# A linear recurrence with hash-routed experts on one core: the lower bound's load on ScalarE's queue, and a new order of emission

## The chip, the core and the metric

The kernel runs on one core of a Trainium2 chip. Five engines work from queues of their own: TensorE (PE in the profile, its weight loads PEld), VectorE (DVE), ScalarE (ACT), GpSimd (POOL) and SyncE (SP, which here only issues transfers). Each engine takes its instructions strictly in the order in which the program emitted them, and waits at one until what it needs is there. The metric is the device time of one execution in microseconds, taken as the median over several runs.

## What is computed

A gated recurrence runs over 4 batches of 5056 steps with 256 channels, and its output, 20224 rows of 256, goes through a mixture of 8 experts. The expert of a row is a hash of its token id, which comes down to the id modulo 8. Each expert is 256 to 1024, relu, 1024 to 256.

```python
sig = 1.0 / (1.0 + np.exp(-f_logit))
f = lower_bound[None, None, :] + (1.0 - lower_bound[None, None, :]) * sig
i = 1.0 - f
for t in range(S):
    h = f[:, t] * h + i[:, t] * x[:, t]
    y[:, t] = h
...
expert_idx = token_ids * np.int64(2654435761) % np.int64(E)
for e in range(E):
    mask = expert_idx == e
    xe = x[mask]
    h = np.maximum(xe @ w1[e], 0.0)
    out[mask] = h @ w2[e]
```

## The kernel before

**Blocks.** Time is cut into 24 blocks: 64, 128, five of 256, two of 128, twelve of 256, one of 128 and two of 64 steps, each for all four batches. For a block, f and x are loaded (`ldf`, `ldx`, lines 831 and 836 early, 1012 later, on SP), turned so that channels lie on partitions, gated (`sig`, `fg`), combined (`st`), scanned on VectorE (`sc`, line 902 early and 1105 later), turned back and copied into `yT`. Blocks 0 to 6 are turned on TensorE (`trf` and `trx`, line 872, `yt`, line 941, and the copies `ye`, lines 955 and 957); later blocks by VectorE's stream transposes. The gate of the early blocks needs `lb_col`, which `load_lb` (line 367) loads.

**Ranks.** A row goes to place expert × capacity + rank in a buffer `srt` in DRAM. Ranks are made in four ranges of columns of 128 tokens: 0 to 6 (blocks 0 and 1), 6 to 46 (blocks 2 to 6), 46 to 78 and 78 to 158. The token ids come by `ids0` to `ids6` (lines 346 and 351) for the first two ranges. `ra0` and `ra6` (lines 438 to 454) make one-hot columns and running sums on VectorE; `rpe` (lines 469 to 475) adds over partitions on TensorE; `rb` and `rc` (lines 480 to 490) give `pos_i`, the places.

**Scatter.** GpSimd writes the rows of a block into `srt` by `si`, one indirect DMA (line 709) for every 128 rows, 114 in all; for some of the later blocks half the rows are sorted on TensorE (line 733) and moved by SP instead. `fill` (line 390, SP) writes zeros into the tiles in the middle of `srt`, reads them from a tile that VectorE writes again in `zfd` (line 402) once the fill has landed, and waits for every scatter emitted ahead of it, since both write `srt`.

**Experts.** `srt` is read in 21 tiles of 128 rows per expert. A read (`rd`, line 1193, SP) needs the fill and the scatters of every block that can reach the tile; tile 0 needs blocks 0 to 2, tiles 2 and 3 need blocks up to 5 and 6, tile 20 block 23. A unit is two tiles (of one expert, or one tile of two experts): `up` (line 1203, TensorE), relu `re` (1212 on ScalarE or 1214 on VectorE), `dn` (1220, TensorE), a copy `oc` into one of four output buffers `ob` (1228 or 1230), and two stores `ro` (line 1234, GpSimd, indirect DMA to the output, 168 in all). The weights come by 16 loads of 0.5 MB from GpSimd's queue (lines 647 and 649; `lw3.1` is the first matrix of expert 3).

**Order.** Every step is a task with an engine and dependencies. The order in which the tasks are emitted, and with it the order in each engine's queue, is a string `ORDER` of 2159 task numbers with one bit that says, for relus, copies and gates that may run on either, whether VectorE takes it. `Plan.order` decodes it; priorities and durations in the tasks play no part then, and dependencies are enforced by semaphores as the instructions need them:

```python
for v in array("H", zlib.decompress(base64.b85decode(ORDER))):
    t = self.tasks[v & 0x7FFF]
    t.on = ("DVE" if v >> 15 else "ACT") if t.alt else next(iter(t.eng))
    out.append(t)
```

Of the kernel before, what the change touches and what calls it, by code (L numbers as in the profile page):

```python
# [55 lines left out]

ORDER = (
    "c-"
    "jTQ1Atvg5CFhYcTa5Fwr$(CZ6}vE*!>&Zwr$(CZQHsk8E}?}#bUKtTgF&B7KznmF<FeDJxj{!vs6Jx){u2zby#Osj~UjOMG3kDiCI_HfW>Emsh}T"
    "A$U3pqK_k{Ah{p!7xGV!p!kPw_bqo5lX2HOqdC-Ej3<j~-EDj4}6Iq&Ia1hQytb5>Ck05O@B=Br2Tgf7VOsprH%!URD*i<%xO<^O0xvUo(6-"  # L60
    ";8QS#mZySjC31`D_83793;KgBih^U@c3=Ua{BgKQ@nTW9x!e!A`b5*v>WtV_12%n=NEx*&eni$QbkvPO!|uE|w+O%Vx5B>?AwR76;kcl3*4~8JuG"
    "Kf(L8|Tgpna{lR?}upB{hzKop?va-HxBiqEX1rOPo;8Adiy<rD}$HCd)97`WuVL5|7Y#e*XuCmxXU2vIIU{8W;tTlTY#N{dYLDq&HV#8TMRwy_eT"
    "o2B(_iQ=)5WHnSSsb39-3V?5AA{fQFDu8MvG`^Mi)TIs$p5g<K`pNN7B-tbXTMkiGoH<1w-_<v|AN~rp-IV8@kAyvXC@La#0v!6Y-"
    "V{_6qA~#F=@>NR)l|HxmZ+_&U|G>c{W~{C+4|>Xh!fHJc$YC(Rnc*gGXk?O^Da#FIjdzf`4Nv0?F^P^kyV4Val=$rf_h9mE#q7)SwQ}$uF{4yrjv"
    "+%k$hOBX7y`25}%?5Wy?*q&$xq&Fk?>JQJ_Pj<URFH6P21u*#+`FB-"
    "g1aiNN7z+3ZVysD|s+nRwq9t`3QO(Ro`C5LEi6mP}H@c7Wi9ASg`MxKx7=b8CSUp!EJC<i{oykPCjCY}J=n>Box>0r9@|4cQ$mapfH%^g;eRc2Xu"
    "^kBG20qb~o-"
    "osQk385SB$eZw<{30*Fo0?L*6CY=KnUpYzPv*VNcvG5}2nzC4P=;lKKISUF#J@Ao6TxPl8cMRue72cr5`$*1RG6v3v%myihW}u*%oRSx#N<;=8b|"
    "^GpKmtsv{063<=1#kKEqt+H+eeXc8f_5QN?sK$L!#9c~!REY&G-"
    "vG_%0m;xWWRlNp+sjIhXT<2U#Lvy;D3yG&oc+blLSO+TIu3}0dnn%gETEH!!IkjV~vO+F|9#i0tz4|_}rNCtOJsh}WafI^T1DnenX#%jYI(}E|3!"  # L70
    "~CAvXZmx?kMNT4*c>&_cqu3X$4pKrFP53o5KUBq<K~TtEl!!I{G{p3%fJcq+T1q}%m7{%-to#1T`cEMOjCGns=!0@*1R`e_-FITy!MV)g>SqLd@="
    "Rlt*-_ZL`4xteC6fBR`HjnJ;W2S#7h3%d^B~T88qkB;ist&aYan=!Ze3mP)+<WJt4kr0F}gGC<-m00_-"
    ";*Om>^V{xTillSyuCz$<gc{N@dzC3J*V&<PTXM4~(tgGP`_C{dlY1|fRE3f>tK+mtq^$R$$PA&|tP$Y86BDxwdxftoA~qy<4DwXMOD+TM`E))2WN"
    "x9tn*Z8F;hx<VS82ZlmMQ45AaWid$P7u_I_&1?HXK06NngPPDE(%MX-rmZUe@LH^))#9`XAhS(p>)0V8tDOPEp)rI*2nLHLkj1uzY&HVM!#_R(ir"
    "ArI5fl{@pdA?KXorb4&;x3V0l-8p+gNn5BcYL<2*pGbF$wD0nJ@~5i+Z-"
    "H?PUM**{}_Y3k%I`ecRdoCrSzkB8foEg66iXwPG@~wB2keI|nw2?sha7u^38-C?c|$0!yKdZ7r6-T-"
    "Yw&sRPg*KB!jK+0x=19|+6f0v`n7Vw9Z+YvDX^YsW&E^>#U|gRx>gY=Cz56pRrKY{>Ss+o8Rk3T4D3y8^a~vwW%;0}ecNuv<g{v02QvJK(*aY?s@"
    "O5Mc|8f?_9Zf?aS0rig>^(XWIN_7Lob!*B#z*jaWn6cTU5G&{$RwsUPc(ZiM%dtjuUXXnFdI0Mt+EX=Uu>`|Bot6{p`B_`M%Vw*SzJH;`$3JdIby"
    "GU$>-QpUYhne;|%(pk-9&CX<b`>muh4zX)W7muQcCVdiFThQ>2rpo7*gkPi+=8oiA)FTn?0q<B--(CNUtG5<!~-~M--<)_B^-"
    "xO@Ceq3+pto+7X!sAam_x4Ug8z>5jX5-@m0KrBlecPV2|1-@CQDLoA$UEAl|@b$RIDlM{&u12EyLri}(s(;Gz9y`--*pqCIRsh-"  # L80
    "2b}eGC0WCixBi*}w4Jt`?uv5AhC8*`MO1jfG#-KiCH+;5(dzbz(o9w%KG7{AC&bws+wNaOCn1XuKmLVPw2*1-"
    "6ozWo!8qqF`+N>SMTc_}NRmZ2#Ej5EmbbpJ7?0aPJ{b_%nDW9@~vV;d7e<3t<_2BA(iea)Zb&Uy5q@0pf*gw?uq|7a}P#7Zqc<UqCJz{)YIN91~z"
    "NOo6dobWG~fV+>4*F<l&&5hKei@~@RH10u$AnQ*blDI>X<m_sU;3ZuB3*hXeXz_zlZ%#Cr~eG%2=!Yo)A^I$XwE@60knaeE`KU4x&1f#p6h%PVYa"
    "b+>SE97#!yfPoA#&)t8=5wiJ*6;?H9}{DFOePcIQc>8=l9gN$ncsa=<*+(dzyhw5OfE~i%B~frkf~)#xlqoL#c{4I<*Le`z9N>uF8ErMab;a+`AQ"
    "UZ9b^rx;%Z`AOe<?)IadiwVnNpszx#fe9n)YMIa@Zu#@Ga_xqG5Ew#GVmMK;A^E*qA{;aJ_3aK&8>SKhV3A+7)x#0su0{wIgYcG$&rb<PcS-"
    "DNZEitVv3cEggczFQ!>$p@koc1Q1exSp;DcEI7TGS+lqF2Ir4AFs-RI9~=XTpBk3dtyDTkBj6WG&oQ8!X(mSbL@zNG2|*bhokVWsDeYVmh0oL%XD"
    "%IPQ|J?8hg10a<LrYT3}zd#D$^9ezKt)6TVDFxZZe8j>T|nB$v9qZW^YS%jGXMAN$L3*b*1uD(vls;s7_ub;j{H0|&YlZjWmsJK+RuE)&Ye?v|X6"
    "`&|sR(yhk-a3O|pCT>OR63KnC5B9}vcvl{9iRBu1Th7A8xCocxAGHQYx!UrkT;-"
    "NvQ@6!U#C7ffuEW`QM;>y`<Zr(gZ^&VI(5=U17*mbFgSgcVcH3P9ZpZcVG|s^txYkX=ZElCFC&#;;xB++LNOuM+sg3y8PmsIt5XMvYTuV6_H@LZY"
    "7$3M@ZlZkX_TWx;1g~LTc@~$4-"  # L90
    "*=nB|EYPn(H+I>xZ3RvUx}OCL;UW};Wzi*RZ(^1Bb*|SVJx*DAGyOWwrU~I;~Sjnj^kT=<}TtS`PglCPh5Pp8CT#1yn#RDb2r(&b06I;{NOI(2|V"
    "d;;$wX3Udr3J4|ltt?uEO9-|-"
    "1nR!_02dWKstp?Z#Yak`u)kI2j6qvbpNf$#B^dx0!0f%@cLyL<S?jg=oTj{4$WVl5>pu8Kwp=#>2DPT^1d<xV>eC-IN_h*$8p`-"
    "NxZIXOnYbq_F+Pvw8(AN=c*s@M1zKcS)|3g|O_c1T3`F|j}E{^1uqFLU|mq$via_A_KMuY63piV_$l_pxZ4oGBC1S9d|a!f*H$^ZGO@5~ZT!GKEj"
    "+Raj=9$>;WIRcsPr)m383LRozt1uC6S?;}$dm5<OTp*Tb;l1fDR{6(3~$EDgTH5KrMR9Z?y$7E7UM_H+w62z&d%HX3?WUtjxd09qLmt-BEj57KfD"
    "tRayMOE1;Jw>7XKD#eL`6-9bK^f?TEbepqjO0{3U(m;=`l=wMq)L>Da#C~^k5W*WDikWA3WS>YTvXSWQH80g_o|BzR}Fj}%1zM}S0$-"
    "bXobp4C4G0_&=;Z7R7wfe%$K3cRF=y6W<&r`l^XeS)PdUim8y;J>f8AdstVPmqST8@tB`8$^H4RaP6K^?sz>D&hK*7Us5#Z3%ru0$`S!j%6{8lR;"
    "?%+yRU=gg-"
    "^#b7FltDxsF><V9espq>C34`)XBG|!m2Z^Qbkl7YD}GIy01t~b)gD$LiMK8N~%6Ij(YgUzAM!X^`*{!D6Lj)L*1yS???Sfhc%(reuh7*DyTmGKkD"
    "T-"  # L100
    "s9~YeezqDw;WXY4r&`pM0_q+LQ3P%Dz5N6~o+>IsGiaQzO=HzbHO7w!wWGCan3|~u(k$PDEVZYJ{=AwH8l*<jb~TYk(KbKW|EDJTNH9drq)9ZJ=J"
    "=kpUM-@zexC2I`l+dYGEMPOU>2>R#k7qEsLiUc8tPA}t=`ivHHC(&(V;;!C$vK?r6r-"
    "LVROmRPBoRL(PTfE*3v>hkCuhj(Q;Z(2PksbG(Uz`&;|<B7C+x_rv?5L?W7%{v2;PLq+K+ftTJjoZKQ*=o379%I!x=-"
    "8nwtTR)=U0t)kU*nlAbybdQeG8G1oy>0Ia-ZSq&?j9N&0={)WB=hPm5jjpTBq3d*kmZ@uMxmv1jgznR2wL~5ASJcJOL%Qns`osPvEub6ffPX-"
    "b=r~>SH~lAiN&9FEJ*HdqhoZqPwV!VLS9Hf8^si~3zf2E2={NL*KGRov==b|C^p<YZ5&xII(L35o|A^@mbcv4o81S89>Bs(&Kc=+4>+jHgpG4oKm"
    "|-W0N2JqFDTh9;evr`j{1abDzo(D%)JN9Q!y-k*)=?s!(K97=R2^4G)6dlhdQNd7ev;Bjb-ajQR7S_w$#t@b1R8XDokC~SDRqX3-"
    ";`5lib$n1>*zYSE~{he>N=Os6OmA(uA#H&tPzEEUL8Xh)v+M4&Zmn+6pLu26Y12toNlbk>*BhCt{9PB=hv~r(&%iugs!A(>bAPJPOIDL%DSYkqia"
    "P}iKwfa=z_YbE~N|Tdb)l@Gu>R5)-7~3-CkGK9U@xlR=T5Zs5|Qhx|8mrTkEd6jYig8chmm^+uC`Z"
)


# [1269 lines left out]
```

## Time and profile before

| | us |
|---|---|
| median of 3 runs | 621.66 |
| lowest and highest | 617.79 and 622.03 |
| the profiled execution | 616.63 |
| its span in the profile | 614.9 |
| TensorE busy | 436.7 |
| VectorE busy | 376.7 |
| GpSimd busy | 315.5 |
| ScalarE busy | 280.1 |

In a timeline row the numbers are start and length in us, then engine, line, operation, output and input, how often it was repeated, and in brackets how long the engine had stood idle before it and what ended that. ACTq and SPq are the issues of transfers on those engines' queues; on GpSimd the length of an indirect DMA row is the time in which it makes the transfer. DMA share is the mean busy share of the 16 DMA engines and can go over 1.

### The profile page before, as it was taken

The numbers are of one execution on the slowest core, as the hardware profiler recorded it, in microseconds if no ns is written. First come the engines' busy times: TensorE is split into PE (matmuls) and PEld (weight loads), VectorE is DVE, ScalarE is ACT, GpSimd is POOL, SyncE is SP. The second block draws the span as 40 slices with busy tenths as digits, with TensorE's granted clock in tenths as the row PEclk, the third lists the DMA queues.
The fourth block names the chain that finished last, engine by engine and source line by source line (L and its number), as shares of the span: only waits on it lengthen the run. The fifth ranks groups of instructions, "written<-read, shape, count | busy, mean of one in ns | idle before, by whom it ended". The sixth has DMA issues, their size and how long they took to land.

```text
span 614.9 us, 10965 instructions
## 1 busy us (share of the span) xinstructions
PE 436.7 (71%) x3750; PEld 356.3 (58%) x3750; DVE 376.7 (61%) x810; ACT 280.1 (46%) x410; POOL 315.5 (51%) x384
## 2 busy tenths in 40 slices
...
GB/s 232 306 201 181 266 245 228 232 180 199 222 255 186 183 202 193 83 211 217 193 163 142 138 137 127 176 125 154 75 182 180 149 80 121 110 104 75 90 87 55
DMA packets 137852, 102.77 MB, mean 167 GB/s; under 512 B 79985, under 2 KB 120925, under 8 KB 137791
## 3 DMA queue, kind: packets, MB, share of 16 engines
...
q10 hardware_dynamic: 3072, 2.35, 1.8%
...
q14 instruction: 30, 0.25, 0.1%
...
## 4 chain that ended last, share of the span: by engine, by line
PE 44%; issue 16%; DMA 11%; another core or an unknown queue 8%; ACT 7%; POOL 6%; DVE 3%; SPq 3%; POOLq 0%; ACTq 0%; DVEq 0%
PE hp L1203 21%; PE op L1220 19%; POOL srt L709 4%; ACT hT L1212 4%; PE so L733 3%; DMA srt<-yT,pos_i 3%; DMA w<-in_moe_w_dram 2%; DMA idt<-in_moe_token_ids_dram 2%; DMA xe<-srt 2%; DMA x_t<-in_x_dram 1%; DMA f_t<-in_f_logit_dram 1%; ACT f_t L1035 1%; DVE y L902 1%; SPq L1193 1%
## 5 line engine op out<-in xcount | busy, mean ns | idle before, releaser
L1234 POOL DMA_INDIRECT out_dram<-ob,row_i x168 | 171.3, 1020 | 207.4 <-ACT ob L1228 133.9
L1203 PE MATMUL hp<-xe,w 128*128 128x256 bf16 (+1 forms) x1664 | 201.1, 273 | 77.5 <-ACT hT L1212 37.6
L1212 ACT ACTIVATE hT<-hp 128x1024 bf16<-128x1024 f32 x138 | 140.0, 1026 | 222.4 <-remote 98.8
L1203 PEld LDWEIGHTS <-w 128*128 128x128 bf16 x1664 | 152.3, 106 | 110.5 <-issue 81.0
L1220 PE MATMUL op<-w,hT 128*128 128x256 bf16 x1344 | 192.7, 294 | 27.3 <-issue 16.4
L1220 PEld LDWEIGHTS <-hT 128*128 128x128 bf16 x1344 | 138.4, 105 | 59.1 <-issue 26.0
L709 POOL DMA_INDIRECT srt<-yT,pos_i x114 | 119.2, 1045 | 84.7 <-issue 31.4
L1088 DVE SCALAR_TENSOR_TENSOR xT<-sT,xT 128x512 f32<-128x512 f32 x56 | 37.8, 679 | 70.3 <-ACT sT L1076 53.8
L1214 DVE TENSOR_SCALAR hT<-hp 128x1024 bf16<-128x1024 f32 x30 | 36.4, 1219 | 70.9 <-remote 29.9
L1105 DVE TENSOR_TENSOR_SCAN y<-sT,y,xT 128x256 bf16<-128x256 f32 (+2 forms) x128 | 79.1, 650 | 0.5
L1228 ACT COPY ob<-op 128x512 f32<-128x512 f32 x65 | 37.4, 585 | 43.7 <-PE op L1220 13.5
L1062 DVE STREAM_TRANSPOSE sT<-f_t 128x512 f32<-128x512 f32 (+1 forms) x64 | 38.8, 621 | 13.6 <-ACT hT L1212 4.5
L1076 ACT ACTIVATE sT<-sT,lb_c,c_c 128x256 f32<-128x256 f32 (+2 forms) x77 | 40.4, 557 | 2.0 <-DVE yT L957 2.0
L733 PE MATMUL so<-yT,oneh 128*128 128x256 bf16 x176 | 29.1, 295 | 13.7 <-issue 13.7
L1062 DVE STREAM_TRANSPOSE xT<-x_t 128x512 f32<-128x512 f32 (+1 forms) x64 | 38.7, 618 | 0.1
L876 ACT ACTIVATE sT<-tf 128x512 f32<-128x512 f32 x23 | 13.7, 596 | 48.1 <-DVE y L902 34.7
L902 DVE TENSOR_TENSOR_SCAN y<-sT,y,xT 128x256 bf16<-128x256 f32 (+1 forms) x48 | 31.5, 690 | 0.2
L1035 ACT ACTIVATE f_t<-f_t 128x1024 f32<-128x1024 f32 (+1 forms) x29 | 29.7, 1029 | 3.7 <-DMA f_t<-in_f_logit_dram 3.7
L872 PE MATMUL tf<-idf,f_t 128*128 128x128 f32 x92 | 20.7, 376 | 11.9 <-DMA f_t<-in_f_logit_dram 7.6
L733 PEld LDWEIGHTS <-oneh 128*128 128x128 bf16 x176 | 17.5, 104 | 19.7 <-issue 17.1
L872 PE MATMUL tx<-idf,x_t 128*128 128x128 f32 x92 | 21.5, 381 | 10.1 <-DVE xT L887 4.7
L941 PE MATMUL yp<-idn,y 128*128 128x128 bf16 x88 | 11.8, 263 | 21.3 <-DVE y L902 12.3
...
## 6 DMA issues: line engine op xcount, KB each, us to landing
...
f_t<-in_f_logit_dram SPq DMA_DIRECT2D x3, 1024.0 KB
x_t<-in_x_dram SPq DMA_DIRECT2D x3, 1024.0 KB
out_dram<-ob,row_i POOLq DMA_INDIRECT x168
...
```

Source lines behind the costliest of these rows:

```text
L709: bi = nc.gpsimd.indirect_dma_start(out=srt[:], out_offset=bass.IndirectOffsetOnAxis(ap=pos_i[:, G0[k] + m:G0[k] + m + 1], axis=0), in_=T[ ...
L733: nc.tensor.matmul(t[:, j, :], lhsT=oneh[:, c, (2 * v + j) * P:(2 * v + j + 1) * P], rhs=T["yT", k][:, 4 + c, :D], start=c == 0, stop=c == 3,)
L872: nc.tensor.transpose(view(t[:, h, :]), T[which, k][:, u * nch + n, h * P:(h + 1) * P], idf[:])
L902: nc.vector.tensor_tensor_scan(yv[:, h, b, :tt], T["sT", un][:, h, c], T["vT", un][:, h, c], init, op0=ALU.mult, op1=ALU.subtract,)
L1062: nc.vector.transpose(o, i_)
L1076: nc.scalar.activation(v, v, AF.Identity, scale=c_c[:, c:c + 1], bias=lb_c[:, c:c + 1])
L1088: nc.vector.scalar_tensor_tensor(x_.rearrange("p s c l -> p (s c l)"), f_.rearrange("p s c l -> p (s c l)"), 1.0, x_.rearrange("p s c l -> ...
L1105: nc.vector.tensor_tensor_scan(yv(T["y", k])[:, cp, :L, s], T["sT", k, u][:, s, n, :], T["xT", k, u][:, s, n, :], init, op0=ALU.mult, op1= ...
L1203: nc.tensor.matmul(hp[:, n * w:(n + 1) * w], lhsT=w1_sb[e][:, h, f * P:(f + 1) * P], rhs=rhs()[:, h, :], start=(h == 0), stop=(h == 1),)
L1212: nc.scalar.activation(hT[:], T["hp", key][:], AF.Relu)
L1220: nc.tensor.matmul(T["op", n][:, h, :], lhsT=lhs(f), rhs=w2_sb[e][:, f, :], start=(f == 0), stop=(f == FF - 1),)
L1234: bi = nc.gpsimd.indirect_dma_start(out=out, out_offset=bass.IndirectOffsetOnAxis(ap=row_i[:, c:c + 1], axis=0), in_=T["ob", n][:, h, :], ...
```

## The change

Three edits. `load_lb` issues its DMA on ScalarE's queue instead of GpSimd's, and its task is named accordingly. The task list gets `early`, which puts the end of the rank of blocks 0 and 1 ahead of the scans of block 2, and that of blocks 2 to 6 ahead of the scans of block 4, in `after`, a list for whatever makes the order; it leads to no instruction and no semaphore. And `ORDER` is another string over the same 2159 tasks.

```diff
 ORDER = (
     "c-"
...
     def load_lb():
         with nc.allow_non_contiguous_dma(reason="256 values"):
-            nc.gpsimd.dma_start(lb_col[:], lower_bound.rearrange("(h p) -> p h", h=2))
+            nc.scalar.dma_start(lb_col[:], lower_bound.rearrange("(h p) -> p h", h=2))
...
-    lbl = add("lb", {"POOL": 0.9}, -101, load_lb, dma=0.8, lat=2.0)
+    lbl = add("lb", {"ACT": 0.7}, -107, load_lb, dma=0.8, lat=2.0)
...
+    early = {2: ranked[0], 4: ranked[2]}
...
-                    after=scs + ([] if f1 else [T["new", k][0]]) + [t for b in bs for t in scans.get((k - 1, b), [])],
+                    after=scs + ([early[k]] if k in early else []) + ([] if f1 else [T["new", k][0]]) + [t for b in bs for t in scans.get((k - 1, b), [])],
```

What the two strings say, decoded, in the stretch where they differ most (a number after the point is the part of a block):

```
ScalarE  before  ids1 ids0 sig0.0 sig1.0 fg0.0 fg1.0 fg0.0 sig1.1 fg1.1 ids2 ids3 ...
         after   lb ids1 ids0 ids2 sig0.0 ids3 fg0.0 sig1.0 ...
GpSimd   before  ... ids6 ip1 ids5 ids4 lw2.1 lw0.1 si1.1 si1.0 si1.0 lw2.0 si0.0 si0.0 si1.1 si2 ...
         after   ... ids5 ids6 ip1 ids4 ip3 lw0.0 si0.0 si0.0 si1.0 si1.0 si1.1 si2 (4) si1.1 si2 (4) lw0.1 si3 ...
GpSimd   before  ... lw5.1 ro0.3 lw4.0 ro0.1 ro0.2 lw5.0 si6.0 ro0.0 si6 (5) si7.0 ...
         after   ... lw4.0 lw2.0 lw3.0 lw5.0 si6 (8) si7.0 si7.1 ro0.0 ro0.1 si7.2 si7.3 si8.0 ...
SP       before  ... ldf5.0 ldx5.0 ldf6.0 fill ldf7.0 ldf7.1 ldx6.0 ldf7.3 ldx7.0 rd0.1 ...
         after   ... ldf4.0 ldx4.0 fill ldf5.0 ldx5.0 lbcl ldf6.0 ldx6.0 ldf7.0 rd0.1 ...
VectorE  before  rb and rc of blocks 0 and 1 behind the scans sc2.3; both halves of ra6 among sc1
         after   fg0.0 ra0 st0.0 sc0.0 sc0.0 yc0 st1.0 ra6 sc1.0 rb ra6 rb sc1.0 rc0 st1.1 sc1.1 sc1.1 rb6 rb6 st2.0 ...
```

The fill has 12 scatters ahead of it in the order before, 9 in the order after. Three units on tile 0 stand ahead of the first unit on tiles 2 and 3 in both orders. From there on the units come in the same order on TensorE, with neighbours swapped and blocks set in at other places: of `up` and `dn` halves, 133 and 116 stand ahead of the last scatter of block 13, 239 and 258 ahead of that of block 20. At the end the scatters of blocks 22 and 23 stand about 5 places further up on GpSimd. Seven of the tasks that may run on either go from VectorE to ScalarE.

## Rows read from the trace of the kernel before

**Rows 1.** Page, part 1: busy time, share of the span, instructions, by engine.
```profile
PE 436.7 (71%) x3750; PEld 356.3 (58%) x3750; DVE 376.7 (61%) x810; ACT 280.1 (46%) x410; POOL 315.5 (51%) x384
```

**Rows 2.** Table by stretches: length, busy PE PEld DVE ACT POOL, clock, DMA share, GB/s.
```profile
0.00:15.40 15.40, 5.88 (x32) 5.08 (x32) 8.20 (x29) 5.14 (x8) 11.12 (x40) 1.00 0.88 232
15.40:30.70 15.30, 5.49 (x34) 4.74 (x35) 4.37 (x12) 1.55 (x3) 0.00 (x0) 0.77 1.06 306
30.70:61.50 30.80, 21.18 (x163) 18.01 (x162) 29.20 (x59) 18.38 (x36) 15.56 (x14) 0.67 0.74 191
61.50:107.60 46.10, 24.38 (x201) 19.78 (x199) 39.07 (x100) 21.29 (x38) 29.80 (x77) 0.65 1.11 246
107.60:186.00 78.40, 48.52 (x421) 40.38 (x422) 55.11 (x131) 40.25 (x60) 46.32 (x46) 0.78 1.22 218
186.00:560.00 374.00, 292.72 (x2528) 235.26 (x2528) 222.81 (x466) 181.35 (x250) 187.94 (x184) 0.86 0.65 150
```

**Rows 3.** Timeline of TensorE: block 5's first transposes, first unit on tiles 2, 3.
```profile
61.70 0.60 PE L872 MATMUL tf<-idf,f_t 128*128 128x128 f32 x4
...
131.00 3.57 PE L1203 MATMUL hp<-xe,w 128*128 128x256 bf16 x16 [6.59 <-DMA xe<-srt]
```

**Rows 4.** Timeline of GpSimd to 120: small load, weights, scatters, first store.
```profile
1.89 0.88 POOL L367 DMA_DIRECT2D lb_col<-in_lower_bound_dram  x1
...
11.08 1.41 POOL L647 DMA_DIRECT2D w<-in_moe_w_dram  x2
42.00 1.29 POOL L709 DMA_INDIRECT srt<-yT,pos_i  x1 [29.51 <-ACT sT L881]
...
60.61 0.97 POOL L709 DMA_INDIRECT srt<-yT,pos_i  x1 [0.30 <-issue]
...
110.72 0.97 POOL L709 DMA_INDIRECT srt<-yT,pos_i  x1 [0.30 <-issue]
...
116.86 1.00 POOL L1234 DMA_INDIRECT out_dram<-ob,row_i  x1 [4.43 <-ACT ob L1228]
```

**Rows 5.** Timeline of VectorE to 80: lower bound, ids, first places, block 5.
```profile
5.32 0.17 DVE L405 TENSOR_SCALAR c_col<-lb_col 128x2 f32<-128x2 f32 x1 [4.09 <-DMA lb_col<-in_lower_bound_dram]
...
27.11 0.19 DVE L438 TENSOR_SCALAR row_t<-idt 128x40 int32<-128x40 int32 x1 [10.09 <-DMA idt<-in_moe_token_ids_dram]
...
40.94 0.17 DVE L490 SCALAR_TENSOR_TENSOR pos_i<-eb_all,r_f 128x6 int32<-128x6 bf16 x1
...
70.05 0.69 DVE L887 SCALAR_TENSOR_TENSOR xT<-sT,tx 128x512 f32<-128x512 f32 x1 [0.63 <-ACT sT L881]
75.53 0.06 DVE L402 MEMSET oneh<- 1x1 bf16 x1 [4.79 <-DMA srt<-oneh]
```

**Rows 6.** Timeline of ScalarE to 50: first activation, ids, last copy of block 2.
```profile
8.68 0.60 ACT L876 ACTIVATE sT<-tf 128x512 f32<-128x512 f32 x1 [4.49 <-PE tf L872]
...
13.46 1.10 ACTq L346 DMA_DIRECT2D idt<-in_moe_token_ids_dram  x2
...
45.59 0.59 ACT L955 COPY yT<-yp 128x512 bf16<-128x512 bf16 x1 [1.75 <-PE tf L872]
```

**Rows 7.** Waits of SP up to 190: waiter, awaited, total us, times, longest.
```profile
SPq L390 <- DMA srt<-yT,pos_i: 16.0, 1, 16.0
```

**Rows 8.** Timeline of SP to 200: the fill.
```profile
62.96 1.03 SPq L390 DMA_DIRECT2D srt<-oneh  x2
```

**Rows 9.** DMA issues: form, queue, count, KB each (page, and 61 to 190).
```profile
f_t<-in_f_logit_dram SPq DMA_DIRECT2D x3, 1024.0 KB
...
srt<-oneh SPq DMA_DIRECT2D x1, 1728.0 KB
srt<-oneh SPq DMA_DIRECT2D x1, 1152.0 KB
```

**Rows 10.** Timeline of the end: last scatter, first unit on tile 20.
```profile
558.08 0.98 POOL L709 DMA_INDIRECT srt<-yT,pos_i  x1 [0.30 <-issue]
...
583.18 1.06 PE L1203 MATMUL hp<-xe,w 128*128 128x128 bf16 x16
```

More of the change, by code (lines that the diff above doesn't have):

```diff
@@ L58 @@
     "c-"
[L59 to L108, printed above, removed]
+    "jrtgMwYl5&+OvRdsCJwr$(CZ6`OoF>@xiZQHhO+qU)I`idokge($ctTwC5+A_{!v6!qLtIwhY?OBYVBdfzykSd7H+OdW#9&5n*u{bO~Ys{hsjRL_"
@@ new lines @@
+    "^2N_sg)|oX4y08JPY0xa_%9;lQSqGMhbz+g3VJ%p<pg(KL2C-HwjHL;>2N{F3L3TEgWe$1-"
+    "Spvrf2O&0sSvHw@mWU;15o{})%7z3zSueJO^=4Vw&>$(x5zJ-tS+-yb3ug=2HnyFO3`PZ$*a9{!7#+-Gi-"
+    "KWndXR+82v)K(>_66qt!6t}GPZ^-4py--Y%SZ(mIMjdSayu<VN2P%pf#JxPOx2U99zb61}B5{L1MNc*vsy*eZg@yi@jo}*d^AN^<k%jjqCxt&o;6"
+    "B!EkmUI1@}@kJ#B@4tvesuq*5#dmJ2O$ltL;EM>5qr3)^zbL=X668vOOgDs5MHTHp>X8}vjHGj*l2YJ{tmOd!RZUl!}-"
+    "rzmE84!=mbFq)XZ}utp%L)a*SR@mhk7u8QKkPY6!K0YC{9h1<=V!Or3KrGOW?xt|vzf&=@pv?rk~33_Cos2JHeQ;2W!!uVQu8#X5I@3dbHP&t2~9"
@@ new lines @@
+    "YU13CB@9v3dKv^+WF4$3mg6PZ-"
+    "J2#?OwnQ}Za&(1Hh@+`e65X9g~c)lPP&&iAO45k7f$t&`VygV<=i<#VJH9yKiyb{l2Ub4KVB_F{vnasSh$;XSZ;-"
+    ")pv&)e`4rVfXo6>n=^u)6#^yUW(_J52GCCLYw|MT3~Uis{O$ns%ldU&lxD2;P9N<@I?fK8iOqjZAmm*lgtO%|M<42JwolgNYwjo%b}Qc>;K$2J<G"
+    "ohXLM=_cB9yGCqW-gkc6*Qoe!zXA;7CzKLhyy-oCBxM|7*UXJxKv3RPm!hz=<c{BcljpYTnW_|fMlL@l&g1jc5WiIl~ydR%n<`}~#^Rm1Qzr@Fzd"
+    "1fNtVkYsqW<G!E!%Pi6#a!W2%~gJ#U*ogQ4W1fin9MNUT;`S8c9RGa!!%Qs<%I*L7%L8k%mQ=J95##1HonAEVT;UGvxCnxop=RSiS6WRV4*p}ql#"
+    "rbx`-i`nxiHQ+~P^XvcfL2+w3vNOg1=W_L`GspUDUNO*BzFNDIf!2~&+#gdFfn-"
@@ new lines @@
+    "7z=$8<RckwrRoB!5QA1=ZCwdHbfF{)IHOm#}rMW06a1G&13VxJT#UM;3c3v6ok_zJ$yEWpd@tRh2gd7%pH#<zVdH8o+t%zMNW8TN(9UK3jWk^``j"
+    "djFD4m$H!Jxn{?oknMc|z|%S%Hgh$AXPY*7VXm@@Fz)PeHi0)Oi>Kv8&U-kYlM!Nj*^AtRK7kEVj?3Dw|-"
+    "Np2I`^tLV(gGc6*NhDsGdQhEJhhL@wWU%F-J~V>_HW##j-"
+    "#n#g0L>wzNMTV3(GoJ*JWwMnvuy~KL@JTmwt~dA5mXd|A&E_DYcOd$fD%KXCd+QK*fch)&1G{#7*r7*p*4W$1eHZqL86*y14V3Fn^W|H&M*$n^Xf"
+    "v28X|}70==Oo)U>r&AE*Tl?K$2zEVu0nLm`<R22CK3&1(bb2X$;Z+YR!ICiXvQX={t&&{{OM{UMtThgvqDt!o?E5HyB%P+ZirgG3wA7K(}?A_8W>"
@@ new lines @@
+    "co-@Mi($e*D_h?#f@0!7F#?8*iC`fRCF}rL18pr6o$N^HXq(#h_787vONt3lN{oWh5JhycoozcCS(Fw%;4hy9-"
+    "JzM?1~XwcbhRbfWS9lZZ8uvg_@Fk42KFDH0#+;r51WMpBi^YwuvIua$<Bo^;q4Z&1j5BqXknMZ0T>8lU=U2U^I)o23sb~$2-"
+    ")s7!mfu=b{(vMu`t4x5o5$u*Z^b2G`k&k!hF~TJ7AaCAvVG(7;Sfp!eS+Cg59tO4#H+AD`wep;-fDlX4^TofG8;D+QV=K-"
+    "uvmWO^mbK#RNOgPJ^A|jp$(y!F0P27Qj7tC&t?&FvIo~Z^dai14m(`ooJ8PJ$Ao13;V=5m~U6Z0{dPZgAVqJU1(pxRk#kv#Y}r1_J&=9EwB|Xz$z"
+    "Fh_Sze8U3^l##Z5SB@53?i3BIU(aKIk4`{5!SvWvt+cmTKHg#9G0*{|XcJc7^Ssy$^-+8g#bd=VeSN3lYjwKwe<d)W3BE5%EA1-"
```

29 lines of the change are left out of this document (added).

## The prediction, made before the change was run

> **What bounds the kernel now.** I read the page's totals first: no engine is full over the span; TensorE, the busiest, has 71% [rows 1]. The table by stretches says why: TensorE is busy 5.49 of 15.30 us in the second stretch, 24.38 of 46.10 in the fourth, but 292.72 of 374.00 from 186 to 560 [rows 2]. So there is a run-in in which the experts have no rows, and a long stage in which they have. The end of the run-in is a row of TensorE's timeline: the first unit on tiles 2 and 3 starts at 131.00, after 6.59 us of waiting for its read of `srt` [rows 3]. That read needs every scatter of blocks 0 to 5, and the last of block 5 issues at 110.72 [rows 4]. From 131 on the units stand in the same order before and after; what moves 131.00 moves the end, unless the DMA engines or later blocks take it back.
>
> Three places in the run-in are late for one reason each. VectorE's timeline: at 27.11 it has stood 10.09 us on token ids, for the first half of `ra6`, with all scans of block 1 queued behind it [rows 5]. ScalarE issued two such loads at 13.46 only, behind activations that waited for data [rows 6], and GpSimd had just put two 0.5 MB weight loads in front at 11.08 [rows 4]. Second, the rank of blocks 0 and 1 is finished at 40.94 [rows 5], and GpSimd's first scatter issues at 42.00 after 29.51 us of idleness [rows 4]; its releaser in that row (an activation) is not what it waited for, the positions are. Third, SP waits 16.0 us on scatters before the zero fill [rows 7], which issues at 62.96 [rows 8], 2.35 us behind the scatter at 60.61 [rows 4], the twelfth and last it must wait for; VectorE then stands 4.79 us at 75.53 on the fill's landing, with the first scan of block 5 behind, whose input was ready at 70.05 + 0.69 = 70.74 [rows 5].
>
> **The change, part by part.** *The id loads.* Block 2's ids now stand ahead of ScalarE's first activation and block 3's right behind it. That one ends at 8.68 + 0.60 = 9.28 [rows 6], so the last ids issue near 9.4 instead of near 13.9. Landing is bounded from both sides: the other small load in these rows, the lower bound, issues at 1.89 [rows 4] and is used at 5.32 [rows 5], 3.4 us; the ids of 13.46 are used at 27.11, 13.65 us. That gives 12.8 to 23.1. VectorE reaches the wait at 27.11 − 10.09 = 17.0, so 4.0 to 10.09 us of the stall go. One weight load is in front instead of two and the issue is 4 us earlier; I take the near end, 9 us gained.
>
> *The rank of blocks 0 and 1.* On TensorE and VectorE it moves from behind the scans of block 2 to among those of block 1: some 0.18 + 0.24 + 0.17 us of VectorE, moved, not added. The two `early` entries bind the planner's order only and emit nothing. Positions are there by about 20 to 25 instead of 41.11, so scatters are limited by the rows of `yT`. Each takes 0.97 with 0.30 between [rows 4].
>
> *The fill.* It now waits for 9 scatters, the last of block 2's rows. The last copy to block 2's `yT` ends at 45.59 + 0.57 or so = 46.2 [rows 6]; 9 us earlier is 37.2, plus 2.35 from scatter to fill gives 39.5. But on SP's queue it is moved in front of both loads of block 5 (and of block 6's). They go out with it: 1728 + 1152 + 2 × 1024 KB [rows 9] are 5.05 MB, 20.5 us at the 246 GB/s of the fourth stretch, 16.5 at the 306 of the second [rows 2]. Block 5's transposes can begin at 56.0 to 60.0 instead of 61.70 [rows 3], and by the same distance as before (70.74 − 61.70 = 9.0) its first scan can at 65.0 to 69.0. Before, it had to wait for 75.53. So block 5 is 6.5 to 10.5 us earlier; the cover that hid the fill's landing is gone, which is why not all of 9 + 4.79 is left.
>
> *The DMA engines.* Up to 131 they moved 15.4·232 + 15.3·306 + 30.8·191 + 46.1·246 + 23.4·218 = 30.6 MB [rows 2], and most stretches have a share near or over 1. Only the third has room: 0.74 and 191 GB/s. Filled to 246 it moves 1.7 MB more, 7.8 us at 218; filled to 306, 3.5 MB, 16 us. With the 6.5 to 10.5 of the chain I take 10 us for the start of the long stage.
>
> *The lower bound's load* goes from GpSimd, where it costs 0.88 us [rows 4], to ScalarE, first in its queue. I price it at nothing on both: GpSimd is then idle for 29.51 us anyway, and ScalarE's first activation starts at 8.68 after 4.49 us of waiting [rows 6]; without that cover it would cost 0.9. The Trainium skill ("DMA: Bandwidth & Descriptors", section "Issuing engines are not separate DMA queues") says that DMAs of all issuing engines run on the same 16 DMA engines, and that issuing on several saves only sequencer time. By that rule the move by itself brings nothing and an earlier fill or scatter only trades places with other transfers, which would make the sum 0; the shares over 1 of rows 2 agree with the rule for two stretches, the 0.74 of the third does not bear out that nothing is left.
>
> *Output rows.* The stores of tile 0 now stand behind all eight scatters of block 6 and two of block 7 on GpSimd; before, three stood ahead of them, the first at 116.86 [rows 4]. Four output buffers hold the units until then, and only three units precede 131.00, so it is hidden unless block 7 is late.
>
> *The rest.* Seven copies or gates go from VectorE to ScalarE (376.7 and 280.1 of 614.9 us busy [rows 1]): nothing. The swaps in the middle change how many unit halves stand ahead of a block's last scatter (133 to 116 for block 13, 239 to 258 for block 20, by the two lists): of TensorE's 374.00 − 292.72 = 81 us idle there [rows 2] I allow 5%, 4 us, either way, and take 0. At the end the last scatter goes some 5 places up, 5 × 1.28 = 6.4 us; but it issues at 558.08 and its tile starts at 583.18 [rows 10], so 0 to 2 us; I take 1.
>
> **Sum.** 616.63 − 10 − 1 = 605.6 us for the profiled execution, whose span is 614.9. The median of the runs is 5.03 above it (621.66): 610.7, so 611.
>
> **Rivals.**
> (a) *Slower: the fill blocks SP.* If the ids land as late as before, `ra6` still stands ahead of the rank's last steps on VectorE, positions come at 41.1, nine scatters at 1.28 need 11.5, and the fill issues at 41.1 + 11.5 + 2.35 = 55. Then block 5's first scan is at 55 + 20.5 + 9 = 84.5, 9 us later than 75.53: 626 for the execution, 631. It decides at a fill issued at 75.53 − 29.5 = 46.0; later than that each us is lost. For it: block 3's ids still stand behind an activation. Against: 39.5 is 6.5 us ahead of that point.
> (b) *Hidden: DMA takes it back.* Scatters and fill come earlier, but reads and weights share the engines whose share is 1.11 and 1.22 from 61.5 to 186 [rows 2]; the gain is under 5 us: 617 to 622. This is also the case in which the change does what it says and nobody waited for it. The rule of the skill cited above is its mechanism. Against: the 0.74 stretch.
> (c) *Full: the lead of the scatters stays.* First scatter 42.00 to about 21, and 131.00 follows to 110: 595.6, 601 by the median; with 2 us at the end and 4 in the middle, 595. For: TensorE waits for reads at 131.00. Against: 16 us by the bytes.
>
> **How the numbers follow.** Forecast (605 to 616) 0.50, (c) 0.12, (b) 0.25, (a) 0.13. The range leaves out the upper part of (a) and the lower tail of (c): 595 to 628; the forecast's own is 605 to 616. About 1%, 6 us, is what a measurement of this kernel tells from no change: faster (under 615.4) has (c) and nearly all of the forecast, with a little of (b): 0.63; same 0.24; slower (over 627.9) 0.13.
>
> **What would show it.** Right: VectorE's stall on ids under 3 us; first scatter before 26; the fill before 46 and no wait of VectorE on it; the first unit on tiles 2 and 3 near 121; the third stretch over 240 GB/s. Wrong: the fill after 46, with waits of TensorE on block 5's loads; TensorE's start near 121 but an end near 617, which would put the loss in the middle; the tile of 583.18 waiting for its read.

## The result

| | before | after |
|---|---|---|
| median, us | 621.85 (4 runs, 617.79 to 624.5) | 586.75 (4 runs, 582.7 to 590.77) |
| the profiled execution, us | 616.63 | 590.77 |
| its span, us | 614.9 | 589.0 |
| TensorE busy, us | 436.7 | 421.2 |

The ratio is 0.944, 95% interval 0.936 to 0.953: 35 us faster, where 11 were forecast and the range ended at 595, 26.7 below the median before. The profiled execution of after is the slowest of its four, that of before lies below all four of its runs, so the two traces differ by 25.9 us only. A run that takes over 1.5% more than the fastest of its kernel counts as slow and is left out of every ratio here, while medians are over all runs.

What follows also needs to know that the chips on which these kernels ran are of two kinds. In four series of runs, each on one chip, the kernel before has a median of 622 to 633 us, in two of 503. The result and the trace of before come from the first kind, whose chips are called slow here, the others fast; ratios are always taken on one chip.

The page of after, part 1 (busy time, share, instructions), answers [rows 1]:

```profile
PE 421.2 (72%) x3750; PEld 349.3 (59%) x3750; DVE 372.8 (63%) x803; ACT 280.8 (48%) x417; POOL 311.4 (53%) x383
```

The table by stretches of after, as in [rows 2]: length, busy PE, PEld, DVE, ACT, POOL, granted clock, DMA share, GB/s.

```profile
0.00:15.40 15.40, 7.67 (x48) 6.22 (x48) 7.33 (x31) 6.35 (x11) 11.23 (x86) 1.00 0.84 224
15.40:30.70 15.30, 8.67 (x85) 7.38 (x84) 13.15 (x30) 9.46 (x20) 5.27 (x5) 0.89 1.13 345
30.70:61.50 30.80, 15.51 (x145) 12.99 (x144) 22.15 (x42) 15.05 (x31) 20.64 (x21) 0.80 0.82 229
61.50:107.60 46.10, 25.06 (x208) 21.17 (x206) 39.80 (x99) 23.02 (x44) 26.36 (x27) 0.76 1.17 257
107.60:186.00 78.40, 56.52 (x459) 45.52 (x460) 63.88 (x140) 39.45 (x55) 44.26 (x43) 0.81 1.08 218
186.00:560.00 374.00, 291.34 (x2618) 241.81 (x2616) 222.90 (x458) 179.06 (x250) 189.93 (x188) 0.89 0.64 149
```

VectorE's second stretch went from 4.37 to 13.15 us busy, and the DMA engines moved 345 GB/s there and 229 in the third, against 306 and 191. The line of 186 to 560 is the one that the prediction did not look into: in the same 374 us TensorE has the same busy time (291.34 against 292.72) and 90 more instructions in it, at a granted clock of 0.89 against 0.86. Over the whole span the same 3750 instructions keep TensorE busy for 421.2 us instead of 436.7, so 15.5 of the 25.9 us between the two spans are the same matmuls, which took less time at a mean granted clock of 0.866 instead of 0.827, and 10.4 us are idle time.

The early steps in after's timelines. VectorE, the wait for ids and the write behind the fill, as in [rows 5]:

```profile
16.18 0.19 DVE L439 TENSOR_SCALAR row_t<-idt 128x40 int32<-128x40 int32 x1 [2.41 <-DMA idt<-in_moe_token_ids_dram]
...
61.38 0.06 DVE L403 MEMSET oneh<- 1x1 bf16 x1
```

GpSimd, the first scatter and the last of block 5 (the 38th), as in [rows 4]:

```profile
20.82 1.09 POOL L711 DMA_INDIRECT srt<-yT,pos_i  x1 [8.12 <-DVE xT L889]
...
88.82 1.39 POOL L711 DMA_INDIRECT srt<-yT,pos_i  x1 [0.30 <-issue]
```

SP, the fill with block 5's loads behind it, as in [rows 8]:

```profile
38.11 1.08 SPq L391 DMA_DIRECT2D srt<-oneh  x2
39.28 1.39 SPq L833 DMA_DIRECT2D f_t<-in_f_logit_dram  x1
40.76 4.49 SPq L833 DMA_DIRECT2D x_t<-in_x_dram  x1
```

TensorE, block 5's first transposes, the last wait ahead of the first unit on tiles 2 and 3, that unit, and a wait behind it, as in [rows 3]:

```profile
59.27 2.79 PE L874 MATMUL tf<-idf,f_t 128*128 128x128 f32 x12 [7.50 <-DMA f_t<-in_f_logit_dram]
...
107.96 1.86 PE L1205 MATMUL hp<-xe,w 128*128 128x128 bf16 x16 [8.71 <-DMA xe<-srt]
111.43 1.89 PE L1205 MATMUL hp<-xe,w 128*128 128x256 bf16 x8 [1.61 <-DMA xe<-srt]
...
142.90 1.86 PE L1205 MATMUL hp<-xe,w 128*128 128x256 bf16 x8 [8.13 <-ACT hT L1214]
```

The stall on ids is 2.41 us, the fill issues 24.85 us earlier and nobody waits for it, and the first unit on tiles 2 and 3 starts at 111.43 instead of 131.00. But counted by TensorE's unit halves (one `up` or one `dn`; there are 336, counted from 0), the lead of 14.5 us at half 12 is 4.1 at half 24, which ends at 149.1 in after: the wait of 8.13 at 142.90 is part of it. It is 2 to 4 us around half 80 (about 236), 14 at half 120, 22 at half 192 and 26.6 at the last. So the profiles say that the early lead was mostly given back and that as much again was gained between 240 and 420 us, where the order differs only in how units, blocks and scatters are interleaved. The experiments had to settle whether that is so.

### The profile page after: what moved, and what is told of

Its sections match the earlier page's. It is cut to its first block, busy times and chain, and to the rows that moved or that the text cites. A ratio compares the mean times of both kernels' runs of the same rounds, so it can differ in the third digit from the quotient of the medians.

```text
span 589.0 us, 10976 instructions
## 1 busy us (share of the span) xinstructions
PE 421.2 (72%) x3750; PEld 349.3 (59%) x3750; DVE 372.8 (63%) x803; ACT 280.8 (48%) x417; POOL 311.4 (53%) x383
## 5 line engine op out<-in xcount | busy, mean ns | idle before, releaser
L1205 PE MATMUL hp<-xe,w 128*128 128x256 bf16 (+1 forms) x1664 | 195.5, 269 | 76.3 <-ACT hT L1214 31.5
L1205 PEld LDWEIGHTS <-w 128*128 128x128 bf16 x1664 | 149.4, 104 | 105.7 <-issue 83.5
L711 POOL DMA_INDIRECT srt<-yT,pos_i x114 | 116.4, 1021 | 90.6 <-issue 27.9
L1230 ACT COPY ob<-op 128x512 f32<-128x512 f32 x58 | 33.6, 587 | 39.7 <-remote 14.8
L1232 DVE COPY ob<-op 128x512 f32<-128x512 f32 x26 | 17.5, 684 | 42.2 <-PE op L1222 17.8
L1078 ACT ACTIVATE sT<-sT,lb_c,c_c 128x256 f32<-128x256 f32 (+2 forms) x66 | 35.5, 564 | 12.9 <-DMA srt<-scr 4.1
L874 PE MATMUL tf<-idf,f_t 128*128 128x128 f32 x92 | 19.0, 349 | 15.4 <-DMA f_t<-in_f_logit_dram 13.1
L874 PE MATMUL tx<-idf,x_t 128*128 128x128 f32 x92 | 18.5, 343 | 12.6 <-ACT yT L957 6.3
L735 PE MATMUL so<-yT,oneh 128*128 128x256 bf16 x176 | 25.2, 288 | 3.1 <-issue 3.1
L1082 DVE TENSOR_SCALAR sT<-sT,c_c,lb_c 128x256 f32<-128x256 f32 (+2 forms) x70 | 25.1, 375 | 0.1
```

The source lines that it names most:

```text
L711: bi = nc.gpsimd.indirect_dma_start(out=srt[:], out_offset=bass.IndirectOffsetOnAxis(ap=pos_i[:, G0[k] + m:G0[k] + m + 1], axis=0), in_=T[ ...
L874: nc.tensor.transpose(view(t[:, h, :]), T[which, k][:, u * nch + n, h * P:(h + 1) * P], idf[:])
L1078: nc.scalar.activation(v, v, AF.Identity, scale=c_c[:, c:c + 1], bias=lb_c[:, c:c + 1])
L1205: nc.tensor.matmul(hp[:, n * w:(n + 1) * w], lhsT=w1_sb[e][:, h, f * P:(f + 1) * P], rhs=rhs()[:, h, :], start=(h == 0), stop=(h == 1),)
L1230: nc.scalar.copy(ob[:], T["op", n][:])
```

## The experiments

All kernels below keep the tasks of the two kernels and differ in the order of emission alone (and, with it, in which engine takes the tasks that may run on two, and in whether the lower bound's load is on ScalarE's or GpSimd's queue). An order that begins with one string and ends with the other emits the first up to a given unit half and then, in the other's order, all that is left.

### The start or the later part

```diff
 e_new24:  ORDER = after, up to TensorE's 24th unit half;  before, from there
 e_old24:  ORDER = before, up to the 24th half;  after, from there
 e_mid:    ORDER = before;  after from half 72 to half 230;  before
 e_old230: ORDER = before, up to half 230;  after, from there
```

> The order after for everything ahead of TensorE's 24th unit half (about 150 us, all of the edits to the early ranks, ids, fill and the lower bound), the order before from there on. Theory S (the start: the lead of the first 150 us is carried to the end): 586 to 592, all 30 to 35 us of the gain. Theory M (the middle: the lead is given back by about 175 us, where the two profiles are only 4 us apart, and more than half of the gain is made later, by where later blocks stand among the units): 608 to 618.

> The reverse: the order before up to TensorE's 24th unit half, the order after from there on. Theory S: 615 to 624, next to nothing. Theory M: 590 to 602, more than half of the gain. If the two parts simply add, the gains of this run and of its counterpart sum to 35 us.

> The order before, but between TensorE's unit halves 72 and 230 (about 220 to 480 us) the order after; the start and the end are those of before. Theory M, with the place read from the profiles (the distance grows from 4 us at half 84 to 22 to 28 us at halves 192 to 228): 598 to 606. Theory S: 618 to 624.

> The order before up to TensorE's unit half 230 (about 480 us), the order after from there on, so only the end is changed. Both theories, since the distance between the profiles does not grow after half 192: 618 to 623. If the end is worth something of its own, 610 to 617.

On one slow chip, the kernel before at 632.55 us (19 runs, 619.45 to 638.64):

| | median, us | less than before, by medians | ratio, 95% interval | less by the ratio |
|---|---|---|---|---|
| e_new24 | 616.47 | 16.1 | 0.987 (0.976 to 0.997) | 1.3% |
| e_old24 | 606.89 | 25.7 | 0.973 (0.962 to 0.983) | 2.7% |
| e_mid | 615.43 | 17.1 | 0.978 (0.970 to 0.986) | 2.2% |
| e_old230 | 627.52 | 5.0 | 0.990 (0.973 to 1.007) | 1.0% |

The ratios are the measure to go by, and they say less than the medians. By them the start brings about 8 us, the later part about 17, the middle about 14 and the end about 6. Theory S falls: the start alone is far from the whole gain, and the later part, for which S had next to nothing, is the larger of the two. Theory M is right on that, but its range for e_old24 (590 to 602) was not reached, and 2.7% is half of the 5.6% of the whole change, not more. The two parts add up to about 4% and leave some 1.5% open. The interval of the end alone takes in nothing.

### Which queue in the middle, and the ids alone

```diff
 e_midpool: ORDER = before;  GpSimd's queue alone as in after between halves 72 and 230
 e_midpead: ORDER = before;  TensorE's, ScalarE's and VectorE's queues as in after between halves 72 and 230
 e_ids:     ORDER = before, with ScalarE's queue
- ids1 ids0 sig0.0 sig1.0 fg0.0 fg1.0 fg0.0 sig1.1 fg1.1 ids2 ids3 ...
+ ids1 ids0 ids2 ids3 sig0.0 sig1.0 fg0.0 fg1.0 fg0.0 sig1.1 fg1.1 ...
```

> The changed kernel itself, beside the next three on the same chip. Chips differ: the kernel before has a median of 621.9 on the chip of the first result and of 632.6 on that of the four runs ahead. All theories: about 0.944 of the kernel before on this chip.

> The kernel before, with GpSimd's queue alone in the new order between TensorE's unit halves 72 and 230 (scatters of blocks moved ahead of output stores); all other queues as before. Theory G (in the middle GpSimd's queue is what held rows back: a scatter that could go stood behind a store that waited for its copy): nearly all of what the whole middle brought, 14 to 17 us. Theory Q (TensorE's own queue held it back: units that waited stood ahead of work that could run): within 4 us of the kernel before.

> The reverse in the same stretch: TensorE's, ScalarE's and VectorE's queues new, GpSimd's and SP's as before. Theory Q: 12 to 17 us faster than the kernel before. Theory G: within 5 us of it.

> The kernel before with one thing moved: ScalarE issues the ids of blocks 2 and 3 ahead of its first activation. The prediction's step: VectorE's stall of 10.09 us on ids falls below 3 us. If that stall is the main part of the early gain (16 us between the medians for everything up to half 24): 8 to 14 us faster. If the late scatters are the main part (positions of blocks 0 and 1 are still made at 30 or later here, the fill still waits for 12 scatters): 0 to 5 us.

These fell on a fast chip, with the kernel before at 503.06 us: e_after 490.78, ratio 0.977 (0.968 to 0.986); e_midpool 503.32, 1.002 (0.998 to 1.006); e_midpead 522.0, 1.042 (1.033 to 1.051); e_ids 490.85, 0.980 (0.971 to 0.989). Neither theory on the middle could be told there, since on this chip nothing of it pays: the ids alone, two transfers moved up by seven tasks, bring the 12 us that the whole change brings (2.0 and 2.3% by the ratios), within the 8 to 14 expected of them. New queues on three engines against old ones on the others cost 19.

### The same on a slow chip

```diff
 e_after2, e_ids2, e_old24b: as e_after, e_ids, e_old24
 e_rankids: ORDER = e_ids, and rpe, rb and rc of blocks 0 and 1 and both id columns moved up, with GpSimd's queue
- si1.1 si1.0 si1.0 lw2.0 si0.0 si0.0 si1.1 ...
+ si0.0 si0.0 si1.1 si1.0 si1.0 lw2.0 si1.1 ...
```

> The changed kernel once more, as the measure for the next three on the same chip. The runs so far came from chips of two kinds: on two of them the kernel before takes 622 and 633 us at a granted clock of 0.83 to 0.85, on one 503 at about 0.9. Slow kind of chip: 0.94 of the kernel before; fast kind: 0.976.

> The kernel before with the ids of blocks 2 and 3 ahead of ScalarE's first activation, again. On a fast chip as measured there, 12 us faster. On a slow chip, theory I (the ids are the whole of the early gain on any chip): 10 to 16 us faster. Theory C (there, what waits for TensorE hides it): under 6 us.

> As the run with the ids, and the end of the rank of blocks 0 and 1, their id columns and the first two scatters moved to where the inputs are ready. If the early ranks add to the ids (the prediction's chain: scatters, fill and block 5 come earlier): 4 to 8 us faster than the ids alone. If the scatters were covered: within 2 us of the ids alone.

> The order before up to TensorE's unit half 24, the order after from there on, again. Theory H (the later part pays only where TensorE reports its results late): on a fast chip within 4 us of the kernel before, on a slow one 17 to 26 us faster as measured there. Theory A (it pays everywhere): 15 us or more on either.

The kernel before is at 628.52 us. e_after2: 589.57, ratio 0.939 (0.932 to 0.946). e_ids2: 621.38, 0.990 (0.982 to 0.997). e_rankids: 625.4 over ten runs from 611.59 to 634.71, without an interval; it shows no gain over the ids. e_old24b: 604.68, 0.965 (0.958 to 0.972). The slow half of theory H holds: the later part brings 3.5% on this chip too, about 22 us (23.8 by the medians). Its fast half was not run by itself; that the later part pays next to nothing there is argued from e_after = e_ids. The start brings what is left of the whole 6.1%, about 16 us; the ids alone bring 6 of them (7 by the medians), between what theories C and I expected. What brings the other 10 is not shown: in e_rankids the first scatter issues at 18.05 instead of the 32.19 of e_ids2, and the time is no better.

What differs between the kinds of chip is seen best on one kernel. ScalarE's waits in e_ids (fast chip), 131 to 480 us: waiter, awaited, total us, times, longest.

```profile
ACT hT L1200 <- PE hp L1191: 56.3, 56, 5.0
ACT hT L1200 <- PE op L1208: 20.1, 11, 4.6
ACT ob L1216 <- PE op L1208: 10.0, 8, 1.9
```

The same view of e_ids2, the same program on a slow chip:

```profile
ACT hT L1200 <- remote: 81.3, 16, 11.1
ACT hT L1200 <- PE hp L1191: 36.0, 30, 3.6
```

TensorE's waits in the same stretch, e_ids:

```profile
PE hp L1191 <- DMA xe<-srt: 25.4, 14, 3.8
```

and e_ids2:

```profile
PE hp L1191 <- ACT hT L1200: 27.4, 9, 8.7
PE op L1208 <- issue: 20.9, 22, 7.3
PE hp L1191 <- issue: 18.9, 22, 7.0
PE hp L1191 <- DVE hT L1202: 10.5, 1, 10.5
```

On the fast chip relus wait for the matmuls that make their input, 1 us at a time (56.3 over 56), and TensorE waits for rows. On the slow chip sixteen relus wait 81.3 us, up to 11.1 each, for something that no recorded event of this core shows ("remote"), TensorE in turn for relus and for nothing that is shown, and hardly for rows. The trace of before, ScalarE's waits over the same 131 to 480, had this too:

```profile
ACT hT L1212 <- remote: 77.3, 17, 9.6
```

The longest of these waits in e_ids2, in the timelines of TensorE, ScalarE and TensorE again:

```profile
463.72 1.04 PE L1191 MATMUL hp<-xe,w 128*128 128x256 bf16 x8
464.59 1.04 PE L1208 MATMUL op<-w,hT 128*128 128x256 bf16 x8
...
474.95 1.02 ACT L1200 ACTIVATE hT<-hp 128x1024 bf16<-128x1024 f32 x1 [11.11 <-remote]
...
476.09 1.87 PE L1191 MATMUL hp<-xe,w 128*128 128x256 bf16 x8 [10.46 <-DVE hT L1202]
```

By the kernel's dependencies a relu waits for TensorE alone: the up half that makes its input, here the one of 463.72, and the down half that frees its buffer. By TensorE's rows, whose ends are modelled, all of that had ended by 465.6; the relu starts 9.3 us later, and TensorE, which needs relus, stands till 476.09. So a result of TensorE came late, or its matmuls ended later than their rows say. The granted clock is 1.00 from 464 to 467 and 0.50 from 470 to 479, and eight matmuls take 1.87 us behind the wait instead of 1.04 ahead of it, so a wait costs more than its length.

Such waits are not chance. ScalarE's rows of two traces from two slow chips with the same order at that place, e_ids2 and e_new24:

```profile
360.14 1.02 ACT L1200 ACTIVATE hT<-hp 128x1024 bf16<-128x1024 f32 x1 [9.39 <-remote]
411.39 1.02 ACT L1200 ACTIVATE hT<-hp 128x1024 bf16<-128x1024 f32 x1 [6.58 <-remote]
```

```profile
356.25 1.02 ACT L1201 ACTIVATE hT<-hp 128x1024 bf16<-128x1024 f32 x1 [9.29 <-remote]
407.61 1.02 ACT L1201 ACTIVATE hT<-hp 128x1024 bf16<-128x1024 f32 x1 [6.69 <-remote]
```

They belong to the same relus, so the order decides where they fall. Their sum goes with the order too. ScalarE's relus over the whole trace, in before, e_ids2, after and e_after2:

```profile
ACT hT L1212 <- remote: 98.8, 21, 9.6
ACT hT L1200 <- remote: 108.5, 21, 11.1
ACT hT L1214 <- remote: 59.9, 16, 10.6
ACT hT L1214 <- remote: 84.1, 19, 7.9
```

In all six traces from slow chips with the old order in the middle (before, e_new24, e_old230, e_ids2, e_rankids, e_loose) the sum is 93 to 112 us, in the six with the new order there (after, e_old24, e_mid, e_after2, e_old24b, e_fill) 60 to 87; in the six traces from fast chips there is no such wait. That is a difference of the right size, but it is not shown to be the cause: ScalarE is not always the engine that others wait for, and e_tight below loses time with a sum of 72.8.

The stretch from 290 to 480 in e_ids2 and, behind it, in e_old24b, which ran on the same chip:

```profile
290.00:480.00 190.00, 140.97 (x1319) 114.05 (x1319) 110.98 (x223) 90.69 (x122) 88.57 (x87) 0.86 0.62 148
```

```profile
290.00:480.00 190.00, 152.73 (x1431) 126.29 (x1429) 124.86 (x251) 98.68 (x138) 97.52 (x96) 0.89 0.64 152
```

The later order gets 1431 TensorE instructions through where the old one gets 1319, 8% more, at a DMA share that is as low. On the fast chip the two orders get 1880 (e_ids) and 1877 (e_after) through.

### What in the later order does it

In the order before, a down half stands on average 5.0 tasks behind its up half on TensorE's queue (halves 130 to the end; 24 of 105 within 3), in the order after 5.5 (10 within 3). A relu lies between the two. Theory D is that this distance is what covers late relus.

```diff
 e_tight:  ORDER = after; behind half 100, 50 down halves moved up on TensorE's queue, e.g.
- dn11.7  5 tasks behind up11.7
+ dn11.7  3 tasks behind up11.7
 e_loose:  ORDER = before; behind half 100, 31 down halves moved down behind the next up half
 e_nopool: ORDER = before up to half 72; from there all queues but GpSimd's as in after
 e_fill:   ORDER = after, VectorE's write behind the fill one place later, and SP's queue
- ldf4.0 ldx4.0 fill ldf5.0 ldx5.0 lbcl ldf6.0 ldx6.0 ldf7.0 ...
+ ldf4.0 ldx4.0 ldf5.0 ldx5.0 lbcl ldf6.0 ldx6.0 fill ldf7.0 ...
```

> The changed kernel with one thing undone: behind half 100, 50 down halves are moved up on TensorE's queue, past one or two tasks, so that they stand closer behind their up half (mean distance behind half 130: 5.5 tasks in the order after, 5.0 before, 4.3 here). Theory D (the later part of the order pays because down halves stand further behind their up halves, which covers relus that are late): on a slow chip 0.97 to 1.00 of the kernel before, 15 us or more of the 35 to 39 lost; on a fast chip within 6 us of the changed kernel (0.976). Theory R (what pays is something else in the later order, as the scatters): 0.94 to 0.95 on a slow chip.

> The reverse: the kernel before, where behind half 100 31 down halves are moved down on TensorE's queue behind the next up half (mean distance behind half 130: 5.7 instead of 5.0); all else as before, the output copies too. Theory D: on a slow chip 8 to 20 us faster than the kernel before; on a fast one within 5 us. Theory R: within 5 us on either, or slower, since the copies now wait.

> From TensorE's half 72 on all queues but GpSimd's as after, GpSimd's as before; ahead of it all as before. On a slow chip the later part as a whole brought 24 to 26 us. Theory G (the scatters' place on GpSimd's queue is the cause): under 8 us faster than before. Theory D: 15 us or more faster.

> The changed kernel with the zero fill back behind the loads of blocks 5 and 6 on SP's queue, 15 scatters ahead of it. If the fill's place is a gain (the stall of 4.79 us it caused before): 4 to 8 us slower than the changed kernel, 0.95 of the kernel before on a slow chip. If the fill ahead of those loads costs as much as it saves (rival a of the prediction in small): as fast as the changed kernel or 1 to 4 us faster.

A slow chip, the kernel before at 628.19 us (14 runs, 614.88 to 640.29):

| | median, us | ratio, 95% interval | TensorE instructions, 290 to 480 us |
|---|---|---|---|
| e_tight | 612.38 | 0.987 (0.978 to 0.995) | 1301 |
| e_loose | 623.72 | 1.010 (0.981 to 1.039) | 1344 |
| e_nopool | 636.09 | 1.029 (1.019 to 1.040) | 1342 |
| e_fill | 591.12 | 0.947 (0.913 to 0.982) | 1444 |

e_tight loses 21 us by the medians against e_fill, which is the changed kernel for this purpose (4% by the ratios; each run of e_tight is slower than each of e_fill), and its rate in the later stretch is back at that of the old order. So closeness of down and up halves can cost what the later part gains. TensorE's waits for relus, 131 to 480 us, agree; e_tight, and behind it e_fill:

```profile
PE hp L1192 <- ACT hT L1201: 27.5, 12, 6.2
PE op L1209 <- ACT hT L1201: 15.5, 9, 3.8
PE hp L1192 <- DVE hT L1203: 3.8, 1, 3.8
```

```profile
PE hp L1192 <- ACT hT L1201: 14.5, 9, 5.1
PE hp L1192 <- DVE hT L1203: 6.9, 2, 5.1
PE op L1209 <- ACT hT L1201: 2.6, 4, 1.1
```

That is 46.8 us against 24.0. But the gain itself does not show in this sum, which is 43.5 in e_ids2, 40.8 in e_old24b and 40.3 in e_after2. And the first experiments speak against the distance as its cause: in e_mid, which has most of the later part's gain, the mean distance behind half 130 is 5.1 (22 of 105 within 3), nearly that of the order before, while e_old230 has 5.4 (13 within 3) and a gain of 1.0%, at most 2.7 by its interval.

e_loose did not bring the 8 to 20 us of theory D. Its median is 4.5 us lower, as theory R has it, but its interval takes in gains and losses, and its output copies still stood where the earlier down halves needed them. e_nopool has the distance of the order after (5.5), and theory D's 15 us of gain did not come: all other queues as after, and the kernel is slower than before, by 8 us by the medians and 18 by the ratio. So the other new queues gain nothing beside GpSimd's old one. It is no proof that scatters are the cause, since stores and scatters there stand in an order made for other neighbours. e_fill lands near the changed kernel's ratio, if with a wide interval, so a gain or loss by the fill's new place is not seen, though VectorE's wait behind the fill is back and longer than before:

```profile
66.69 0.06 DVE L390 MEMSET oneh<- 1x1 bf16 x1 [12.11 <-DMA srt<-oneh]
```

```diff
 e_tight2: ORDER = after; every second of the 50 moves of e_tight (24)
 e_pool72: ORDER = before; GpSimd's queue alone as in after from half 72 to the end
```

> As the run with 50 down halves moved up, with every second of them only (24), so that the mean distance behind half 130 is 4.9, that of the order before (5.0). Theory D at its own dose: on a slow chip half of what the 50 cost, 8 to 14 us slower than the changed kernel, 0.955 to 0.965 of the kernel before. If the 50 cost time only because they went beyond the order before: within 4 us of the changed kernel, 0.94 to 0.945.

> The kernel before with GpSimd's queue alone in the new order from TensorE's half 72 to the end. Theory G alone (scatters further up are enough): 12 us or more faster on a slow chip. If GpSimd's queue pays only together with the queues that feed it (without it the others were 8 us slower than the kernel before): within 6 us of the kernel before, or slower.

They fell on a fast chip (before: 502.89): e_tight2 494.21, 0.982 (0.977 to 0.986), e_pool72 510.79, 1.015 (1.009 to 1.021). There 24 closer down halves cost little, if anything, against the changed kernel's 0.977 on the other fast chip, as theory D wants it; GpSimd's queue alone costs 8 us. What either does on a slow chip at this dose was not measured.

## Why the prediction was wrong

**What held.** The direction, and the early chain nearly number for number up to block 5. Ids: a stall under 3 us was asked for, 2.41 came. First scatter before 26: 20.82. Fill forecast at 39.5, issued at 38.11; block 5's first transposes forecast at 56.0 to 60.0 and waiting for loads, they began at 59.27 after 7.50 us on them; VectorE's stall of 4.79 [rows 5] is gone. The small load moved to ScalarE cost nothing that shows.

**The step that failed: "The rest".** "of TensorE's 374.00 − 292.72 = 81 us idle there [rows 2] I allow 5%, 4 us, either way, and take 0". The later part, which that term has at nothing, is worth 17 to 22 us by the ratios (24 to 26 by the medians) on the kind of chip on which before was profiled (e_old24, e_old24b). The swaps were taken as neutral because the units come in the same order; that says nothing of what the interleaving does to the waits between engines. And the trace of before had the reason to ask: 81 us idle in a stretch with a DMA share of 0.65 [rows 2] is not a stage bound by TensorE's work, and what interrupted it (77.3 us of relus waiting for "remote") stands in no term of the prediction. Nor does the granted clock of 0.86 [rows 2], which falls where TensorE stands, as around 470 in e_ids2: 15.5 us of the profiled gain are busy time of the same matmuls. The stage's rate could move, and 336 halves make much of a small change: 20 us is 0.06 us for each.

**Terms mis-sized.** The start was priced at 10; it is worth about 8 us by e_new24 (interval 2 to 15) and about 16 by e_after2 against e_old24b. So the price is about right, but by luck, since the path to it was wrong. The step stopped at block 5's first scan and carried its lead of 6.5 to 10.5 to the end of the run-in, and from there, by "what moves 131.00 moves the end", to the end; the last scatter of block 5 issued 21.9 us earlier (88.82 against 110.72 [rows 4]) and the first unit on tiles 2 and 3 19.6, so rival (c) was right on the run-in and the forecast of 121 was not, and then the lead shrank: 14.5 us at half 12, 4.1 at half 24. Why it shrank was not tested. The third stretch reached 229 GB/s and not 240, while the second rose to 345, which the sum on the DMA engines took for full at 306.

The end was priced at 1; the run gives about 6 us by the ratio (5.0 by the medians) with an interval from a loss of 4 to a gain of 17, so it stays open.

**The rivals.** (a) did not happen: the fill was 8 us ahead of the point at which it decides. (b) is wrong in total on either kind of chip. The Trainium skill ("DMA: Bandwidth & Descriptors", section "Issuing engines are not separate DMA queues") has all issuers share 16 DMA engines, so that another issuer saves sequencer time only. The runs don't contradict that and it decided nothing: e_ids changed no issuer and moved two small transfers up their own queue, and that was worth 12 us on a fast chip. (c) gave 601 and at most 595 by the median; 586.75 came, but by another way: by the runs about half of the gain, and in the two traces most of it, was made behind the place where (c) made it.

**What stays open.** Why TensorE's results come late to relus on some chips, what in the later order makes its 17 to 22 us, and what beside the ids makes the start's. Shown is that moving down halves closer (beyond the order before, 4.3 against 5.0) costs 21 us there, and that the other new queues gain nothing without GpSimd's; not shown is the cost of the distance at the old order's own dose on a slow chip. That the distance is the cause of the gain is not shown either, and e_mid, e_old230 and e_nopool speak against it.
